# Turning the PSUM banks of a block's result, and converting weights in parts of 1024 columns: a state-space scan fused with two feed-forward layers

## The chip, the cores and the metric

The kernel runs on one core of one Trainium2 chip. The metric is the device time of one execution in microseconds (us). TensorE is called PE below, VectorE DVE, ScalarE ACT, GpSimd POOL, and SP is the engine that issues the DMAs.

## The reference, cut to what matters

```
# 1. scan over 4 sequences x 8 heads, 768 tokens each, in chunks of 32 tokens
L  = exp(cum_i - cum_j) * causal;  M = (C @ B.T) * L
y  = M @ x + (C @ state) * exp(cum)          # state is carried from chunk to chunk
# 2. two feed-forward layers on 3072 tokens x 256
h = x @ w_in;  g = maximum(0.01*h, h);  x   = g @ w_out       # 256 -> 2048 -> 256
h = x @ w_in2; g = maximum(h, 0);       out = (g * g) @ w_out2
```

The outputs are fp32. The eight-byte weights are handed over as they lie in memory and turned into fp32 pairs on the chip.

## The kernel before, in words

The 3072 tokens are cut into 12 **pieces** of 256. Each piece is scanned (`scan_piece`): DVE and ACT scale and decay the inputs, PE makes the small products S and Y, SP spreads four tiles into block-diagonal form by DMA (L321: `kbd`, `xbh`, `xbl`, `sbd`), and at the end ACT and DVE write the piece's result as a high and a low part, `yh` (L400) and `yl` (L401).

The two layers work on **blocks** (`Phase`) in the order of the table ORDER: six blocks of layer 1 with one piece each (256 columns), called blocks 0 to 5 here, then nine blocks with two pieces each (512 columns) of layers 2 and 1 by turns. A block has 16 slices of the 2048 hidden rows. For a one-piece block they go in 8 groups of two slices. A group is: `hmm`, 12 matmuls into a PSUM tile `hp` (L423 to L425, three buffers); `act`, which makes `gh` and its low part `gl` (L433, L434, L439); and `omm`, 12 matmuls into the block's result `o` (L451, L452, L456), two groups behind `hmm`. The result has two halves of 128 rows, d = 0 and 1. After a block of layer 1, `finish` copies each half to `yh` on ACT (L464) and subtracts for `yl` on DVE (L465). Until both are done, that half of `o` can't be written again.

Each product of fp32 values is three matmuls of high and low parts, so each weight matrix must be split once into a high and a low part. That is the **weight conversion**. A part of a matrix is loaded (L127, by SP), then goes through two ACT operations (L136, L139), two DVE operations (L147, L148), one ACT copy that makes the high part `wh` (L161) and one DVE subtraction that makes the low part `wl` (L162). In the code before, a part has 512 columns of eight-byte values (512 KB), the staging pool `wp` has 8 such buffers, and the steps `split_w`, `split_w1`, `split_w2` each run one part behind the other. Of the last matrix the low parts replace staging buffers (`w2o` tiles, from the same pool), and its last six parts have 256 columns and go through a single buffer called `all`, which the reductions over a sequence (L275, L277) use too.

Layer 1's weights (`1i` and `1o`) are converted on demand within block 0; from then on `w_step` is called `W_PACE` times a group. The order in which an engine's instructions stand is made by a scheduling layer out of the order of the calls and of the buffers that come free; each engine then runs its queue strictly in order. So an instruction that waits holds up all that stand behind it on its engine, on SP too.

Of the kernel before, what the change touches and what calls it, by code (L numbers as in the profile page):

```python
# [18 lines left out]
P = 128  # L19
BATCH, H, S, D, N = 4, 8, 768, 32, 16  # L20
T = 32
TP = 256
# [6 lines left out]
DM, FF = H * D, 2048  # L29
KI, KO = DM // P, FF // P  # L30
# [9 lines left out]

ENDS = [0, 12, 28, 44, 60, 76, 132, 156, 176, 216, 236, 280]
LAG = {1: 2, 2: 3}
W_AHEAD = 4
W_FROM, W_PACE = 16, 0.4


@with_exitstack
def ssd_moe_kernel(ctx: ExitStack, tc: tile.TileContext, in1, in2, w1i, w1o, w2i, w2o, out):
# [6 lines left out]
    nc = tc.nc  # L55

    cp = ctx.enter_context(tc.tile_pool(name="cp", bufs=1))
    sp = ctx.enter_context(tc.tile_pool(name="sp", bufs=1))
    sm = ctx.enter_context(tc.tile_pool(name="sm", bufs=2))
    wp = ctx.enter_context(tc.tile_pool(name="wp", bufs=8))  # L60
    yp = ctx.enter_context(tc.tile_pool(name="yp", bufs=2))
    ap_ = ctx.enter_context(tc.tile_pool(name="ap", bufs=2))
    ph = ctx.enter_context(tc.tile_pool(name="ph", bufs=3, space=bass.MemoryType.PSUM))
    po = ctx.enter_context(tc.tile_pool(name="po", bufs=1, space=bass.MemoryType.PSUM))
    pz = ctx.enter_context(tc.tile_pool(name="pz", bufs=1, space=bass.MemoryType.PSUM))


# [30 lines left out]
    w_last = {}  # L98
# [3 lines left out]

    def w_out(nm, m, c):
        if nm == "2o":
            t = w_last[m // 2]
            return t[:, 0, m % 2, c], t[:, 1, m % 2, c]
        return w_hi[nm][:, m, c], w_lo[nm][:, m, c]


    wq = [(nm, c, None) for c in range(8) for nm in ("1i", "1o")]  # L110
    wq += [("2i", c, None) for c in range(8)] + [("2o", c, None) for c in range(5)]
    wq += [("2o", c, j) for c in range(5, 8) for j in range(2)]
    w_loaded, w_half, w_full, w_done = [], [], [], set()

    def load_w():
        nm, c, j = wq.pop(0)
        if nm[1] == "i":
            sl = (slice(None), slice(None), slice(c * 256, c * 256 + 256))
        elif j is None:
            sl = (slice(None), slice(2 * c, 2 * c + 2), slice(None))  # L120
        else:
            sl = (slice(None), slice(2 * c + j, 2 * c + j + 1), slice(None))
        if j is None:
            st = wp.tile([P, 2, 256], I64, tag="w", name="wst")
        else:
            st = sp.tile([P, 1, 256], I64, tag="all", name="wst")
        nc.sync.dma_start(st, w_dram[nm][sl])  # L127
        w_loaded.append((nm, c, j, sl, st))

    def split_w():  # L130
        nm, c, j, sl, st = w_loaded.pop(0)
        v = st.bitcast(I32).rearrange("p k (f two) -> p k f two", two=2)
        w0, w1 = v[:, :, :, 0], v[:, :, :, 1]


        nc.scalar.activation(w1.bitcast(F32), w1.bitcast(F32), AF.Copy, scale=2.0**-112)  # L136


        nc.scalar.activation(  # L139
            w0, w0.bitcast(U32), AF.Copy, scale=2.0**-29 * (1 - 2.0**-14), bias=7.5 * 2.0**-14 - 0.5  # L140
        )
        w_half.append((nm, c, j, sl, w0, w1))

    def split_w1():

        nm, c, j, sl, w0, w1 = w_half.pop(0)
        nc.vector.scalar_tensor_tensor(w0, w1, 3, w0, ALU.logical_shift_left, ALU.bitwise_or)  # L147
        nc.vector.scalar_tensor_tensor(w0, w1, -(1 << 31), w0, ALU.bitwise_and, ALU.bitwise_or)  # L148
        w_full.append((nm, c, j, sl, w0.bitcast(F32)))

    def split_w2():

        nm, c, j, sl, w = w_full.pop(0)
        if nm == "2o":
            if c not in w_last:
                w_last[c] = wp.tile([P, 2, 2, 256], F32R, tag="w", name="w2o")
            k = slice(0, 2) if j is None else slice(j, j + 1)
            h, l = w_last[c][:, 0, k], w_last[c][:, 1, k]
        else:
            h, l = w_hi[nm][sl], w_lo[nm][sl]  # L160
        nc.scalar.activation(h, w, AF.Copy)  # L161
        nc.vector.tensor_tensor(l, w, h.bitcast(F32), ALU.subtract)  # L162
        if j != 0:
            w_done.add((nm, c))

    def w_step():
        if w_full:
            split_w2()
        if w_half:
            split_w1()  # L170
        if w_loaded:
            split_w()
        if wq:
            load_w()
# [8 lines left out]
    def load_piece(p):  # L183
        v = sp.tile([P, U * (N + T + D)], F32, tag="in1", name="in1")
        w = sp.tile([P, U * 2 * T], F32, tag="in2", name="in2")
        nc.sync.dma_start(v, in1[p])
        nc.sync.dma_start(w, in2[p])
        return part(v, N + T, D), part(v, 0, N), part(w, T, T), part(v, N, T), part(w, 0, T), part(w, 0, T + N)
# [215 lines left out]
    class Phase:  # L404
# [38 lines left out]
        def omm(self, ms):  # L443
            n = self.n
            if self.o is None:
                self.o = [po.tile([P, 512], F32, tag=f"o{d}", name=f"o{d}")[:, :n] for d in range(2)]
            gs = [self.g.pop(m) for m in ms]
            for m, (gh, gl) in zip(ms, gs):
                for d in range(2):
                    wh, wl = w_out(self.wo, m, slice(d * P, d * P + P))  # L450
                    nc.tensor.matmul(self.o[d], wl, gh, start=(m == 0), stop=False)  # L451
                    nc.tensor.matmul(self.o[d], wh, gh, start=False, stop=False)  # L452
            for m, (gh, gl) in zip(ms, gs):
                for d in range(2):
                    wh, _ = w_out(self.wo, m, slice(d * P, d * P + P))
                    nc.tensor.matmul(self.o[d], wh, gl, start=False, stop=(m == KO - 1))  # L456

        def finish(self):
            n = self.n
# [25 lines left out]
    loaded = {0: load_piece(0)}  # L485
    for _ in range(W_AHEAD):
        load_w()
# [32 lines left out]
    def second(lag):  # L520
        while len(pend) > lag:
            ph_, ms = pend.pop(0)
            ph_.omm(ms)
            if ms[-1] == KO - 1:
                ph_.finish()
# [3 lines left out]
    for layer, p0, n in ORDER:  # L529
        g, o = divmod(p0, 2)  # L530
        ph_ = Phase(layer, p0, n, *(t[:, o : o + n] for t in ys[g]))
        for m in range(0, KO, 2 // n):
            ms = list(range(m, m + 2 // n))
            while (ph_.wo, m // 2) not in w_done:
                w_step()
            ph_.hmm(ms)
            pos += 2
            ph_.act(ms)
            step_to(due(pos))
            pend.append((ph_, ms))  # L540
            second(LAG[n])
            if pos >= W_FROM:
                acc += W_PACE
            while acc >= 1:
                acc -= 1
                w_step()
# [52 lines left out]
```

## Time and profile before

| | |
|---|---|
| time, median of 3 runs (range) | 653.15 us (650.84 to 655.68) |
| profiled execution, its own time | 652.62 us |
| its span, first to last instruction | 650.8 us |
| PE busy | 595.4 us, 91% of the span, 4248 matmuls |
| DVE busy | 422.6 us, 65% |
| ACT busy | 358.9 us, 55% |
| HBM read and written | 36.83 MB and 3.15 MB |

How to read it: the shares are means over very different stretches. In the first 40 us the PE has little to do; from about 240 us on it is busy nearly without a break, while DVE and ACT have slack; between lies the stretch in which scans, weight conversion and the one-piece blocks share DVE and ACT. The times of single instructions and waits come from views of the same execution.

### The profile page before, as it was taken

What the parts mean: (1) busy time and instruction counts of PE and PEld (TensorE: products, weight loads), DVE (VectorE), ACT (ScalarE), POOL (GpSimd) and SP (SyncE); (2) the same over time, 40 slices, a digit from 0 to 9 for tenths busy, and PEclk for the clock granted to TensorE, in tenths of its full rate; (3) what the DMA queues carried; (4) which work ended last, traced back from release to release, by engine and by line L of the source; (5) the groups of instructions that cost most, each with busy time, mean ns of one, the idle gap of its engine ahead of it and who ended that gap; (6) DMA issues with size and microseconds to landing.
All of it is one profiled execution on the core that took longest, in us unless ns stands there. A gap on an engine that the chain in (4) does not pass through costs nothing.

```text
span 650.8 us, 10980 instructions
## 1 busy us (share of the span) xinstructions
PE 595.4 (91%) x4248; PEld 508.0 (78%) x4248; DVE 422.6 (65%) x735; ACT 358.9 (55%) x639; POOL 5.1 (1%) x14
## 2 busy tenths in 40 slices
PE   0276978899999999999999999999999999999997
PEld 0276868899999978888878888878888888788885
DVE  7998889899676587567673676652465322544553
ACT  5986867686555545555554455553444433544442
POOL 3000000000000000000000000000000000000000
PEclk9998879899999999999999999999999999999999
DMA  9647664633633423022332022030000000000000
GB/s 335 213 84 227 206 147 133 184 39 97 132 92 70 125 70 48 9 74 50 57 82 56 33 26 49 33 63 3 1 10 1 26 7 0 1 1 1 34 0 32
DMA packets 111251, 46.45 MB, mean 71 GB/s; under 512 B 94304, under 2 KB 100064, under 8 KB 111200
## 3 DMA queue, kind: packets, MB, share of 16 engines
q1 hardware_dynamic: 111200, 45.76, 27.6%
q8 instruction: 33, 0.54, 0.3%
q14 instruction: 18, 0.15, 0.1%
HBM read 36.83 MB, written 3.15 MB: 61 GB/s over the span
## 4 chain that ended last, share of the span: by engine, by line
PE 72%; DVE 14%; ACT 5%; DMA 5%; issue 3%; SPq 1%; DVEq 0%; ACTq 0%
PE o L451 12%; PE hp L423 12%; PE hp L424 11%; PE hp L425 11%; PE o L452 11%; PE o L456 11%; DMA wst<-w2o 2%; DVE gl L439 2%; DVE lt L199 1%; DMA all<-in 1%; DMA in<-in 1%; DVE wst L147 1%; DVE e L205 1%; DVE wst L148 1%; ACT gh L433 1%
## 5 line engine op out<-in xcount | busy, mean ns | idle before, releaser
L439 DVE TENSOR_TENSOR gl<-t,gh 128x512 fp32r<-128x512 f32 x192 | 132.3, 689 | 133.9 <-ACT t L434 80.5
L433 ACT ACTIVATE gh<-hp 128x512 fp32r<-128x512 f32 x96 | 57.2, 596 | 91.8 <-PE o L452 67.2
L423 PE MATMUL hp<-yl,wh1i 128*128 128x256 f32 (+1 forms) x288 | 95.9, 333 | 10.3 <-DVE yl L401 6.8
L438 ACT CAST gh<-t 128x512 fp32r<-128x512 f32 x96 | 59.6, 621 | 68.9 <-DVE t L437 53.8
L451 PE MATMUL o<-gh,wl1o 128*128 128x256 f32 (+1 forms) x288 | 90.1, 332 | 6.3 <-DVE yl L465 3.5
L437 DVE TENSOR_TENSOR t<-t 128x512 f32<-128x512 f32 x96 | 66.1, 689 | 45.5 <-ACT t L436 45.2
L425 PE MATMUL hp<-yh,wl1i 128*128 128x256 f32 (+1 forms) x288 | 94.3, 327 | 0.0
L424 PE MATMUL hp<-yh,wh1i 128*128 128x256 f32 (+1 forms) x288 | 94.1, 327 | 0.0
L436 ACT ACTIVATE t<-hp 128x512 f32<-128x512 f32 x96 | 57.4, 598 | 59.6 <-PE hp L425 57.3
L452 PE MATMUL o<-gh,wh1o 128*128 128x256 f32 (+1 forms) x288 | 88.8, 327 | 0.0
L451 PE MATMUL o<-gh,w2o 128*128 128x512 f32 x192 | 76.4, 398 | 1.3 <-DVE yl L465 1.3
L423 PE MATMUL hp<-yl,wh2i 128*128 128x512 f32 x192 | 76.2, 397 | 0.0
L425 PE MATMUL hp<-yh,wl2i 128*128 128x512 f32 x192 | 75.6, 394 | 0.0
L424 PE MATMUL hp<-yh,wh2i 128*128 128x512 f32 x192 | 75.5, 393 | 0.0
L452 PE MATMUL o<-gh,w2o 128*128 128x512 f32 x192 | 74.8, 389 | 0.0
L423 PEld LDWEIGHTS hp<-yl,wh1i 128*128 128x128 f32 x288 | 56.8, 197 | 15.7 <-DVE yl L401 7.0
L451 PEld LDWEIGHTS o<-gh,wl1o 128*128 128x128 f32 x288 | 56.0, 194 | 11.8 <-DVE yl L465 3.7
L456 PE MATMUL o<-gl,wh1o 128*128 128x256 f32 (+1 forms) x288 | 62.2, 323 | 0.5 <-DVE gl L439 0.5
L424 PEld LDWEIGHTS hp<-yh,wh1i 128*128 128x128 f32 x288 | 56.8, 197 | 4.4 <-issue 0.2
L456 PE MATMUL o<-gl,w2o 128*128 128x512 f32 x192 | 60.2, 393 | 0.0
L425 PEld LDWEIGHTS hp<-yh,wl1i 128*128 128x128 f32 x288 | 56.5, 196 | 4.4
L452 PEld LDWEIGHTS o<-gh,wh1o 128*128 128x128 f32 x288 | 56.0, 194 | 3.9
(124 smaller groups left out, 932.7 us busy)
## 6 DMA issues: line engine op xcount, KB each, us to landing
in<-in SPq DMA_DIRECT2D x12, 640.0 KB, 4.5
in<-in SPq DMA_DIRECT2D x12, 512.0 KB, 3.3
all<-in SPq DMA_DIRECT2D x15, 384.0 KB, 3.5
wst<-w1i SPq DMA_DIRECT2D x8, 512.0 KB, 6.7
wst<-w1o SPq DMA_DIRECT2D x8, 512.0 KB, 6.6
wst<-w2i SPq DMA_DIRECT2D x8, 512.0 KB, 4.7
out_t<-ob SPq DMA_DIRECT2D x12, 256.0 KB, 2.2
wst<-w2o SPq DMA_DIRECT2D x5, 512.0 KB, 5.1
```

The lines of the kernel that those rows point to most:

```text
L147: nc.vector.scalar_tensor_tensor(w0, w1, 3, w0, ALU.logical_shift_left, ALU.bitwise_or)
L423: nc.tensor.matmul(hp, wh, self.xl[:, :, k], start=(k == 0), stop=False)
L424: nc.tensor.matmul(hp, wh, self.xh[:, :, k], start=False, stop=False)
L425: nc.tensor.matmul(hp, wl, self.xh[:, :, k], start=False, stop=(k == KI - 1))
L433: nc.scalar.activation(gh, hp, AF.Lrelu)
L436: nc.scalar.activation(t, hp, AF.Relu)
L437: nc.vector.tensor_tensor(t, t, t, ALU.mult)
L438: nc.scalar.copy(gh, t)
L439: nc.vector.tensor_tensor(gl, t, gh.bitcast(F32), ALU.subtract)
L451: nc.tensor.matmul(self.o[d], wl, gh, start=(m == 0), stop=False)
L452: nc.tensor.matmul(self.o[d], wh, gh, start=False, stop=False)
L456: nc.tensor.matmul(self.o[d], wh, gl, start=False, stop=(m == KO - 1))
```

## The change

Four things are changed together.

1. A one-piece block's result no longer takes a 256-column half of each of two PSUM banks, but both halves of one bank. The pool `po` has one tag with two buffers, so blocks take the banks in turn. Only the first matmul into the bank has the start flag. A two-piece block still takes both banks, one for each half of the rows.
2. A weight part has 1024 columns (1 MB) instead of 512, but for the first four (columns 0 to 511 of `1i` and of `1o`), which keep 512, and for the last eight, which have 256. That makes 24 parts in place of 35. The pool `wp` has 4 buffers of double size, of which each of the first four parts fills half of one.
3. `split_w` and `split_w1` are one step, so the conversion has two steps a part.
4. Two parts are loaded ahead instead of four, and a `w_step` is called 0.3 times a group instead of 0.4.

```diff
-W_AHEAD = 4
-W_FROM, W_PACE = 16, 0.4
+W_AHEAD = 2
+W_FROM, W_PACE = 16, 0.3
...
-    wp = ctx.enter_context(tc.tile_pool(name="wp", bufs=8))
+    wp = ctx.enter_context(tc.tile_pool(name="wp", bufs=4))
...
-    po = ctx.enter_context(tc.tile_pool(name="po", bufs=1, space=bass.MemoryType.PSUM))
+    po = ctx.enter_context(tc.tile_pool(name="po", bufs=2, space=bass.MemoryType.PSUM))
...
-    wq = [(nm, c, None) for c in range(8) for nm in ("1i", "1o")]
-    wq += [("2i", c, None) for c in range(8)] + [("2o", c, None) for c in range(5)]
-    wq += [("2o", c, j) for c in range(5, 8) for j in range(2)]
-    w_loaded, w_half, w_full, w_done = [], [], [], set()
+    wq = [(nm, c, n) for c, n in ((0, 2), (2, 2), (4, 4), (8, 4), (12, 4)) for nm in ("1i", "1o")]
+    wq += [("2i", c, 4) for c in range(0, KO, 4)] + [("2o", 0, 4), ("2o", 4, 4)]
+    wq += [("2o", c, 1) for c in range(8, KO)]
+    w_loaded, w_half, w_done = [], [], set()
...
+        pool, tag, size = (sp, "all", 256) if n == 1 else (wp, "w", 1024)
+        st = pool.tile([P, size], I64, tag=tag, name="wst")[:, : 256 * n]
...
-        w_half.append((nm, c, j, sl, w0, w1))
-    def split_w1():
-        nm, c, j, sl, w0, w1 = w_half.pop(0)
         nc.vector.scalar_tensor_tensor(w0, w1, 3, w0, ALU.logical_shift_left, ALU.bitwise_or)
         nc.vector.scalar_tensor_tensor(w0, w1, -(1 << 31), w0, ALU.bitwise_and, ALU.bitwise_or)
-        w_full.append((nm, c, j, sl, w0.bitcast(F32)))
+        w_half.append((nm, c, n, sl, w0.bitcast(F32)))
...
     def w_step():
-        if w_full:
-            split_w2()
         if w_half:
-            split_w1()
+            split_w2()
...
-                self.o = [po.tile([P, 512], F32, tag=f"o{d}", name=f"o{d}")[:, :n] for d in range(2)]
+                o = [po.tile([P, 512], F32, tag="o", name="o") for _ in range(self.n // TP)]
+                self.o = [o[0][:, d * n : d * n + n] for d in range(2)] if n == TP else o
...
-                    nc.tensor.matmul(self.o[d], wl, gh, start=(m == 0), stop=False)
-                    nc.tensor.matmul(self.o[d], wh, gh, start=False, stop=False)
+                    f = m == 0 and (d == 0 or n > TP)
+                    nc.tensor.matmul(self.o[d], wl, gh, start=f, stop=False, skip_group_check=True)
+                    nc.tensor.matmul(self.o[d], wh, gh, start=False, stop=False, skip_group_check=True)
...
-            while (ph_.wo, m // 2) not in w_done:
+            while (ph_.wo, ms[-1]) not in w_done:
                 w_step()
```

The change moves instructions on every engine. In the rows below a line number of the changed kernel is 8 lower than before in the scan and 4 lower from `omm` on, so L351 of before is L343 now, L401 is L393, L465 is L461.

**PE, where block 0 ends and block 1 begins.** `hp` is the hidden tile, `o0`, `o1` (before) and `o_1096` (now) block 1's result, `kbd` and `S` belong to the scan of piece 2. Before:

```order
L424 MATMUL hp_1310<-yh_337,wh1i_110 128x256
L425 MATMUL hp_1310<-yh_337,wl1i_111 128x256
L451 MATMUL o0_1161<-gh_987,wl1o_113 128x256
L452 MATMUL o0_1161<-gh_987,wh1o_112 128x256
L351 LDWEIGHTS kbd_95
L351 MATMUL S_1050<-ch_950,kbd_95 128x32
```

Now:

```order
L416 MATMUL hp_1056<-yh_333,wh1i_110 128x256
L417 MATMUL hp_1056<-yh_333,wl1i_111 128x256
L447 MATMUL o_1096<-gh_930,wl1o_113 128x256
L448 MATMUL o_1096<-gh_930,wh1o_112 128x256
L447 MATMUL o_1096<-gh_930,wl1o_113 128x256
L448 MATMUL o_1096<-gh_930,wh1o_112 128x256
```

Before, block 1's result is begun after the hidden tiles of its first six groups, with the scan's S right behind. Now it is begun after three groups' hidden tiles, and results and hidden tiles alternate from there on.

**ACT, in the scan of piece 0, ahead of the first block.** `d1s` and `shl` carry the piece's states, `wst` are staging buffers of weight parts; `wst_395` is the part of `1o` for slices 4 to 7. Before:

```order
L136 ACTIVATE wst_365<-wst_365 128x512
L380 ACTIVATE d1s_233<-Y_240,kk_158 128x32x8
L161 ACTIVATE wh1o_112<-wst_126 128x512
L139 ACTIVATE wst_365<-wst_365 128x512
L385 CAST shl_296<-stt_290 128x16x16
```

Now:

```order
L136 ACTIVATE wst_357<-wst_357 128x1024
L139 ACTIVATE wst_357<-wst_357 128x1024
L372 ACTIVATE d1s_229<-Y_236,kk_154 128x32x8
L136 ACTIVATE wst_395<-wst_395 128x1024
L377 CAST shl_292<-stt_286 128x16x16
```

The first operation on `wst_395` now stands between `d1s` and `shl`, so `shl` waits for the landing of that part.

**DVE, the last rows ahead of `yl` of piece 2**, with which block 2 begins. Before:

```order
L147 SCALAR_TENSOR_TENSOR wst_893<-wst_893 128x512
L353 TENSOR_TENSOR e1_1454<-in1_1246,e1_1454 128x512
L344 SCALAR_TENSOR_TENSOR xl_1488<-in1_1246,sc_1149,xh_1451 128x512
L148 SCALAR_TENSOR_TENSOR wst_893<-wst_893 128x512
L215 MEMSET d1s_1576 128x32
L465 TENSOR_TENSOR yl_338<-o0_1161,yh_337 128x256
L334 SCALAR_TENSOR_TENSOR kmx_1444<-in2_1247,sc_1149,him_1396 128x512
L401 SCALAR_TENSOR_TENSOR yl_1362<-Y_1194,fac_945,yh_1361 128x512
```

Now:

```order
L345 TENSOR_TENSOR e1_1388<-in1_1188,e1_1388 128x512
L461 TENSOR_TENSOR yl_334<-o_1096,yh_333 128x256
L142 SCALAR_TENSOR_TENSOR wst_1115<-wst_1115 128x1024
L336 SCALAR_TENSOR_TENSOR xl_1422<-in1_1188,sc_1084,xh_1385 128x512
L143 SCALAR_TENSOR_TENSOR wst_1115<-wst_1115 128x1024
L326 SCALAR_TENSOR_TENSOR kmx_1378<-in2_1189,sc_1084,him_1338 128x512
L393 SCALAR_TENSOR_TENSOR yl_1296<-Y_1136,fac_888,yh_1295 128x512
```

Two conversions stand among these rows in both programs, of 512 columns before and of 1024 now; the second half of block 1's finish (L461) has moved ahead of `yl`.

## Rows read from the trace of the kernel before

**Rows 1.** The page, part 1: busy us, share of the span, instructions.
```profile
PE 595.4 (91%) x4248; PEld 508.0 (78%) x4248; DVE 422.6 (65%) x735; ACT 358.9 (55%) x639; POOL 5.1 (1%) x14
```

**Rows 2.** Stretches, us: busy PE, PEld, DVE, ACT, POOL; clock, DMA share, GB/s.
```profile
37.40:116.10 78.70, 64.01 (x616) 60.02 (x616) 71.48 (x140) 57.76 (x107) 0.00 (x0) 0.89 0.61 162
116.10:232.80 116.70, 111.15 (x1165) 107.74 (x1165) 92.66 (x167) 72.68 (x141) 0.00 (x0) 0.98 0.44 106
232.80:650.80 418.00, 413.69 (x2348) 335.11 (x2348) 225.53 (x346) 199.41 (x344) 0.00 (x0) 1.00 0.13 29
112.90:119.80 6.90, 3.67 (x17) 3.67 (x18) 6.31 (x13) 3.38 (x7) 0.00 (x0) 0.51 0.37 38
```

**Rows 3.** Waits of PE, 40 to 240 us: us in total, times, longest.
```profile
PE o L451 <- DVE yl L465: 4.8, 2, 3.5
PE hp L423 <- DVE yl L401: 4.0, 1, 4.0
...
PE o L451 <- DVE wl1o L162: 2.6, 2, 2.3
```

**Rows 4.** Timeline of PE: start us, us, instruction, idle before it.
```profile
37.37 0.58 PE L423 MATMUL hp<-yl,wh1i 128*128 128x256 f32 x1 [2.78 <-DVE yl L401]
...
90.10 0.58 PE L451 MATMUL o<-gh,wl1o 128*128 128x256 f32 x1 [3.54 <-DVE yl L465]
...
116.14 0.58 PE L423 MATMUL hp<-yl,wh1i 128*128 128x256 f32 x1 [4.02 <-DVE yl L401]
...
232.79 0.50 PE L451 MATMUL o<-gh,w2o 128*128 128x512 f32 x1 [1.25 <-DVE yl L465]
```

**Rows 5.** Busy time as in rows 2, `yl` of piece 0 to `yl` of piece 2.
```profile
36.57:115.33 78.76, 64.04 (x616) 60.05 (x616) 71.54 (x142) 57.94 (x108) 0.00 (x0) 0.90 0.62 163
```

**Rows 6.** Groups by line and shape, DVE, 37.4 to 115.2 us: count, busy us, mean ns.
```profile
L148 DVE SCALAR_TENSOR_TENSOR wst<-wst 128x512 int32<-128x512 int32 x16 | 10.5, 684 | 0.0
L147 DVE SCALAR_TENSOR_TENSOR wst<-wst 128x512 int32<-128x512 int32 x15 | 9.8, 681 | 0.0
...
L162 DVE TENSOR_TENSOR wl1o<-wst,wh1o 128x512 fp32r<-128x512 f32 x6 | 4.1, 690 | 2.7 <-ACT wh1o L161 2.6
```

**Rows 7.** Timeline of DVE: start us, us, instruction.
```profile
47.40 1.29 DVE L147 SCALAR_TENSOR_TENSOR wst<-wst 128x512 int32<-128x512 int32 x2
48.60 0.69 DVE L148 SCALAR_TENSOR_TENSOR wst<-wst 128x512 int32<-128x512 int32 x1
...
114.36 0.39 DVE L465 TENSOR_TENSOR yl<-o,yh 128x256 fp32r<-128x256 f32 x1
...
115.33 0.75 DVE L401 SCALAR_TENSOR_TENSOR yl<-Y,fac,yh 128x512 fp32r<-128x512 f32 x1
```

**Rows 8.** Groups by line and shape, the whole span, conversion at two sizes.
```profile
L136 ACT ACTIVATE wst<-wst 128x512 f32<-128x512 f32 x29 | 19.5, 674 | 1.7 <-DMA wst<-w1i 1.6
...
L136 ACT ACTIVATE wst<-wst 128x256 f32<-128x256 f32 x6 | 2.6, 442 | 5.6 <-DMA wst<-w2o 5.6
...
L148 DVE SCALAR_TENSOR_TENSOR wst<-wst 128x256 int32<-128x256 int32 x6 | 2.5, 424 | 0.1
```

**Rows 9.** Waits of DVE, 36.6 to 115.3 us: us in total, times, longest.
```profile
DVE wl1o L162 <- ACT wh1o L161: 2.6, 3, 1.5
DVE m L293 <- PE S L290: 2.0, 1, 2.0
```

**Rows 10.** Timeline of ACT in the scan of piece 0.
```profile
29.33 0.66 ACT L385 CAST shl<-stt 128x256 f16<-128x256 f32 x1 [0.80 <-DVE stt L223]
```

**Rows 11.** Timeline of SP's queue: a load of `1o`.
```profile
20.83 0.33 SPq L127 DMA_DIRECT2D wst<-w1o  x1
```

**Rows 12.** The page, part 6: DMA issues, KB each, median us to landing.
```profile
in<-in SPq DMA_DIRECT2D x12, 640.0 KB, 4.5
...
wst<-w1o SPq DMA_DIRECT2D x8, 512.0 KB, 6.6
wst<-w2i SPq DMA_DIRECT2D x8, 512.0 KB, 4.7
```

More of the change, by code (lines that the diff above doesn't have):

```diff
@@ L104, in w_out @@
         if nm == "2o":
-            t = w_last[m // 2]
-            return t[:, 0, m % 2, c], t[:, 1, m % 2, c]
+            t = w_last[m // 4]
+            return t[:, 0, m % 4, c], t[:, 1, m % 4, c]
         return w_hi[nm][:, m, c], w_lo[nm][:, m, c]
-    wq = [(nm, c, None) for c in range(8) for nm in ("1i", "1o")]
-    wq += [("2i", c, None) for c in range(8)] + [("2o", c, None) for c in range(5)]
-    wq += [("2o", c, j) for c in range(5, 8) for j in range(2)]
-    w_loaded, w_half, w_full, w_done = [], [], [], set()
+    wq = [(nm, c, n) for c, n in ((0, 2), (2, 2), (4, 4), (8, 4), (12, 4)) for nm in ("1i", "1o")]
+    wq += [("2i", c, 4) for c in range(0, KO, 4)] + [("2o", 0, 4), ("2o", 4, 4)]
+    wq += [("2o", c, 1) for c in range(8, KO)]
+    w_loaded, w_half, w_done = [], [], set()
     def load_w():
-        nm, c, j = wq.pop(0)
+        nm, c, n = wq.pop(0)
+        pool, tag, size = (sp, "all", 256) if n == 1 else (wp, "w", 1024)
+        st = pool.tile([P, size], I64, tag=tag, name="wst")[:, : 256 * n]
         if nm[1] == "i":
-            sl = (slice(None), slice(None), slice(c * 256, c * 256 + 256))
-        elif j is None:
-            sl = (slice(None), slice(2 * c, 2 * c + 2), slice(None))
-        else:
[L122 to L126, printed above, removed]
+            st = st.rearrange("p (k f) -> p k f", k=KI)
+            sl = (slice(None), slice(None), slice(c * P, (c + n) * P))
+        else:
+            st = st.rearrange("p (k f) -> p k f", f=DM)
+            sl = (slice(None), slice(c, c + n), slice(None))
         nc.sync.dma_start(st, w_dram[nm][sl])
-        w_loaded.append((nm, c, j, sl, st))
+        w_loaded.append((nm, c, n, sl, st))
     def split_w():
-        nm, c, j, sl, st = w_loaded.pop(0)
+        nm, c, n, sl, st = w_loaded.pop(0)
         v = st.bitcast(I32).rearrange("p k (f two) -> p k f two", two=2)
@@ L141, in split_w @@
         )
-        w_half.append((nm, c, j, sl, w0, w1))
-    def split_w1():
-        nm, c, j, sl, w0, w1 = w_half.pop(0)
         nc.vector.scalar_tensor_tensor(w0, w1, 3, w0, ALU.logical_shift_left, ALU.bitwise_or)
         nc.vector.scalar_tensor_tensor(w0, w1, -(1 << 31), w0, ALU.bitwise_and, ALU.bitwise_or)
-        w_full.append((nm, c, j, sl, w0.bitcast(F32)))
+        w_half.append((nm, c, n, sl, w0.bitcast(F32)))
     def split_w2():
-        nm, c, j, sl, w = w_full.pop(0)
+        nm, c, n, sl, w = w_half.pop(0)
         if nm == "2o":
[L155 to L158, printed above, removed]
+            g, o = divmod(c, 4)
+            if g not in w_last:
+                w_last[g] = wp.tile([P, 2, 4, DM], F32R, tag="w", name="w2o")
+            h, l = w_last[g][:, 0, o : o + n], w_last[g][:, 1, o : o + n]
         else:
@@ L162, in split_w2 @@
         nc.vector.tensor_tensor(l, w, h.bitcast(F32), ALU.subtract)
-        if j != 0:
-            w_done.add((nm, c))
+        w_done.update((nm, m) for m in range(c, c + n))
     def w_step():
-        if w_full:
+        if w_half:
             split_w2()
-        if w_half:
-            split_w1()
         if w_loaded:
@@ L455, in omm @@
                     wh, _ = w_out(self.wo, m, slice(d * P, d * P + P))
-                    nc.tensor.matmul(self.o[d], wh, gl, start=False, stop=(m == KO - 1))
+                    nc.tensor.matmul(self.o[d], wh, gl, start=False, stop=(m == KO - 1), skip_group_check=True)
         def finish(self):
```

## The prediction

> **What bounds the kernel now.** I read the busy times first, then stretches, then the PE's waits, then the queue of the engine that ends them. PE is busy 595.4 us of 650.8 [rows 1]. From 232.8 us to the end it is busy 413.69 of 418.00 at a granted clock of 1.00, and the last 4 us are the final copy and store [rows 2]; nothing in the change touches that stretch. From 116.1 to 232.8 us it is busy 111.15 of 116.70. So only two places can give much: the time before the first block, and the stretch from 37.4 to 116.1 us, blocks 0 and 1, where PE is busy 64.01 of 78.70 us and the clock is 0.89.
>
> In that stretch DVE is busy 71.48 of 78.70, so PE is not its bound. The PE's waits say the same: the largest end with DVE's `yl`, 4.0 us on the scan's (L401) and 4.8 us on the finish's (L465), and 2.6 us with DVE's `wl1o` [rows 3]. Single rows place them: at 90.10 us PE has stood 3.54 us for block 0's finish, at 116.14 it has stood 4.02 us for piece 2's `yl`, at 232.79 it has stood 1.25 us for block 5's finish [rows 4]. By 116.14 PE has run out of everything: blocks 0 and 1 are complete, and block 2 needs piece 2. **So the wait that ends last is `yl` of piece 2**, an instruction in DVE's queue, and what PE gains earlier it loses there. The change is worth what it does to the time of that instruction, plus what it does after it.
>
> **Part 1, the banks in turn.** The 3.54 us at 90.10 go: block 1 no longer needs block 0's bank. What is late next is piece 2's `yl`, so by itself this buys nothing, except through DVE: one idle wait of DVE, 2.0 us for `m` from PE's S (L290) [rows 9], came about because that S stood in PE's queue behind block 1's `omm`, which stood still. I count these 2.0 us as gained. The order of PE supports it: `omm` of block 1 now follows its third group.
>
> A wait is added: both halves lie in one bank now, and the order shows the second ACT copy (L464 for d = 1) waiting for the first DVE subtraction, which it didn't. Behind it on ACT stand the next group's `gh` and `t`. It happens six times, a copy and a subtraction late at most, and up to block 4 PE has another bank to go on with: zero, with at most 0.8 us on the other side. Block 5 is followed by a two-piece block, which takes both banks, one of them block 5's; its 1.25 us [rows 4] may go or double, and I leave them.
>
> **Part 2, larger parts, on DVE.** Between `yl` of piece 0 and `yl` of piece 2 lie 78.76 us, of which DVE is busy 71.54 and idle 7.2 [rows 5]. Conversion takes 15 + 16 + 15 instructions of 512 columns there (of the last 15, 6 stand in the row of `wl1o` and 9 in two like it) [rows 6]. Back to back they begin 0.60 us apart (47.40, 48.60 after two [rows 7]), so 46 x 0.60 = 27.6 us. In the order of the changed kernel 8 + 9 + 9 = 26 of 1024 columns stand there: because a part comes whole, and because the parts run further ahead, more of the conversion falls before piece 2. A larger one is priced from two sizes: 424 ns at 256 columns [rows 8] and 684 at 512 [rows 6], 260 for 256 more, so 684 + 520 = 1204 ns, and 1.12 us from one to the next by the same overlap of 0.08. 26 x 1.12 = 29.1, which is **1.5 us more**. Between these two points the changed order also has one scan instruction of 512 columns (`cl`) that stood before, 0.67 us by the row of L401 less the overlap, one more half of a finish, 0.31 us (both [rows 7]), and five of one or three columns, 0.5 us together as an estimate from the shortest half above. **Sum: 3.0 us more for DVE.**
>
> Against it stands the idle time. The 2.0 us of part 1 go. The 2.6 us in which DVE waited for ACT's `wh1o` [rows 9] should go too, since ACT has less to do: at 674 and 442 ns for 512 and 256 columns [rows 8] one of 1024 takes 1138, 210 less than two, and each subtraction now has a longer one of another part ahead of it to hide the copy. That is -4.6, with 2.6 us of idle time kept. Bounds: none of the 7.2 goes (+3.0 net), or all (-4.2 net).
>
> **Part 3, the first block's start.** Before, `shl` runs on ACT at 29.33 [rows 10] and block 0 begins at 37.37 [rows 4]. Now the first operation on `wst_395`, 1.14 us, stands ahead of `shl`. Its load goes into the buffer of another part of `1o` and can be issued when that part's `wl` is done, at the place where SP issued its next `1o` load before, 20.83 [rows 11]. It holds `shl` up once it lands after 29.33 - 1.14 = 28.2, that is once it takes over 7.4 us. Loads of 512 KB took 4.7 and 6.6 us, one of 640 KB 4.5 [rows 12]. So 1 MB takes from 4.7 (no slower than half of it) to 13.2 (two of the slow ones in a row), which costs 0 to 5.8 us. I take 8.0, between the slow 6.6 and twice 4.7: **0.6 us**. The Trainium skill (DMA: Bandwidth & Descriptors, Bandwidth) gives 6.15 us for one load of 1 MB from HBM. By that the part would land at 27.0, this term would be 0 and the sum 0.6 lower. Its fit in the section on a DMA's anatomy, 2.0 us plus the bytes at 436 GB/s, makes 3.2 us of 512 KB; the trace has 4.7 and 6.6, so I don't use it.
>
> The rest of the DVE's queue ahead of the first `yl` changes by less than 0.3 us: three more conversions of 512 columns, 1.6 net after merging, come in; one `wl` (0.60), `cl` (0.67) and five short ones go out.
>
> **Part 4, afterwards.** From 116.1 to 232.8 DVE is busy 92.66 of 116.70 and PE idle 5.55 [rows 2]. The last eight parts cost three more short instructions each way and the earlier ones less: zero, bounded by those 5.55 us below and by 1 us above. Fewer steps called (0.3 a group) do no harm: twelve steps bring 12 parts until the first two-piece block, which covers all of `2i` and most of `2o`.
>
> **Sum:** +3.0 - 4.6 + 0.6 = -1.0 us on the profiled execution's 652.62 (a span of 650.8 and 1.8 around it): **651.6 us**. That execution lies 0.5 below the median of the three runs, 653.15, well within their 650.84 to 655.68. About 1% (6.5 us) is what I take as distinguishable from no change.
>
> **Rivals.**
>
> *DVE's queue closes up.* All 7.2 us of idle time go, so -4.2; block 2 begins without PE standing still long before it, so the low clock behind that wait (0.51 from 112.9 to 119.8 [rows 2]; 3.67 us of PE's work at half speed) gives 1.8 back; the 1.25 us at 232.79 go, and half of the other 4.3 us of PE's idle time after 116.1. -9.4 in all: 643.2. For it: one cause, PE standing before L465, is removed, and idle time on DVE comes from PE. Against: PE has slack all through this stretch, so DVE's queue alone must shorten.
>
> *ACT stands before loads of 1 MB* (slower). The place is `shl`; it decides from a landing time over 7.4 us. At 9.4 to 13.2 us it costs 2.0 to 5.8, in the middle 3.9 on block 0's start. The later parts of `1o` then land late as well and the 2.6 us on `wh1o` stay: 3.0 - 2.0 + 3.9 = +4.9, so 657.5. For it: 512 KB took 6.6 us here. Against: fewer loads share the engines at the start.
>
> *The banks only move the wait.* PE waits at 116 in place of 90 and the conversions come out even: 652.6.
>
> *The clock.* In blocks 0 and 1 the granted clock is 0.89, and it is 0.51, the lower of its two levels (1.2 GHz) nearly throughout, in the 6.9 us around PE's wait of 4.02 us [rows 2, 4]. If at each of the five borders between one-piece blocks PE waited briefly so that the clock fell in the same way, each would cost the 1.8 us worked out above, 9 in all: 660.6. The Trainium skill (TensorE: Matmul & The Clock Gate, A second HAM failure mode) tells of a kernel whose cycling through PSUM banks made short PE gaps between groups and the clock swing. The trace here speaks against it: the hidden tiles turn through three banks from 232.8 us on and the clock stays at 1.00 [rows 2].
>
> **Chances.** Forecast 0.45, the queue closes up 0.20, ACT before loads 0.20, the wait only moves 0.11, the clock 0.04. Faster by over 1% (below 646.6) is most of the second and a tail of the first: 0.19. Slower by over 1% (above 659.7) is the clock and the upper third of the third: 0.13. The rest, 0.68, is within 1%. The range reaches down to 644, which cuts off the lower half of the fast rival, and up to 659, which cuts off the clock and the latest landings. The forecast alone, by its bounds of -4.2 and +3.0 and runs 1.5 us apart either way, would be 647 to 657.
>
> **What would show it.** Right: no wait of PE for L465 near 90 us, one for L401 near 115; conversions of 1024 columns near 1.2 us on DVE and 1.14 on ACT; DVE idle about 2.6 us between the two `yl`; `shl` within a microsecond of 29.3. Wrong: ACT idle before L136 with a DMA as its releaser, or block 0 beginning after 39 us (the load's rival); block 2 beginning before 112 us (the queue closing up); low clock at block borders behind 120 us.

## The result, and the profile after

| | before | after |
|---|---|---|
| time, median (range), runs | 652.25 us (650.84 to 655.68), 4 | 660.34 us (659.10 to 660.74), 4 |
| profiled execution, its span | 652.62, 650.8 us | 660.56, 658.8 us |

The ratio is 1.0113 [1.0069, 1.0157]; run again later it was 1.0117 [1.0091, 1.0143]. The change makes the kernel 1.1% slower, 7.4 us by this ratio; the forecast was 651.6 in a range of 644 to 659, no change. Two executions, one of e10 (3256 us) and one of e13 (754.5 us), took far longer than all others of their kernels and are left out of the ratios.

The page of the changed kernel, part 1, answers to [rows 1]: PE has about as much to do as before.

```profile
PE 597.3 (91%) x4248; PEld 510.4 (77%) x4248; DVE 421.9 (64%) x702; ACT 356.4 (54%) x606; POOL 5.1 (1%) x14
```

Stretches of it, with the columns of [rows 2]: blocks 0 and 1; block 2 to the wait at 241.48; the rest; `yl` of piece 0 to `yl` of piece 2, as [rows 5]; and two stretches of low clock.

```profile
37.40:117.95 80.55, 63.13 (x616) 59.64 (x617) 74.72 (x129) 61.06 (x89) 0.00 (x0) 0.89 0.63 173
117.95:241.48 123.53, 114.89 (x1168) 111.25 (x1169) 90.70 (x157) 69.36 (x135) 0.00 (x0) 0.95 0.41 94
241.48:658.80 417.32, 412.72 (x2344) 334.37 (x2344) 223.70 (x343) 199.20 (x344) 0.00 (x0) 1.00 0.13 28
36.62:117.06 80.44, 63.13 (x616) 59.61 (x616) 74.61 (x129) 60.95 (x90) 0.00 (x0) 0.90 0.62 173
110.40:124.10 13.70, 7.16 (x61) 7.12 (x62) 11.90 (x16) 7.35 (x14) 0.00 (x0) 0.50 0.49 76
192.30:199.20 6.90, 4.69 (x19) 4.02 (x20) 2.97 (x11) 0.97 (x2) 0.00 (x0) 0.51 0.37 73
```

The last stretch is as long as before (418.00), the first 1.85 us longer (78.70), the middle one 6.8 longer (116.70). So in these two executions most of the loss lies behind block 2's start, where the forecast had put zero. PE's larger waits in the execution after the change:

```profile
112.53 0.18 PE L388 MATMUL Y<-qh,sbd 128*128 128x32 f16 x1 [4.10 <-DMA sbd<-t]
...
117.95 0.55 PE L415 MATMUL hp<-yl,wh1i 128*128 128x256 f32 x1 [4.41 <-DVE yl L393]
...
194.51 0.38 PE L282 MATMUL S<-ident,mx 128*3 128x128 f32 x1 [4.52 <-DVE mx L269]
...
241.48 0.47 PE L447 MATMUL o<-gh,w2o 128*128 128x512 f32 x1 [1.77 <-DVE yl L461]
```

The wait at 90.10 of [rows 4] is gone, and block 2 starts 1.81 us later (117.95 for 116.14). Block 5's border (241.48) has 1.77 us in place of 1.25. New is 194.51: the S of sequence 2's reduction (L282), which finds the scales of pieces 6 to 8. Before, the same matmul (L290) waited 0.72 us:

```profile
198.23 0.27 PE L290 MATMUL S<-ident,mx 128*3 128x128 f32 x1 [0.72 <-DVE mx L277]
```

Its operand did not come later than before: the reduction that it waits for began at 197.22 us before and at 193.50 after, so it came 3.7 us earlier. PE came to it earlier still. In PE's order it stands behind 935 block matmuls (`hmm` and `omm`) before and behind 867 after, 68 fewer, and PE stands until the reduction arrives. The reduction in its turn waited for a load:

```profile
193.50 0.95 DVE L269 TENSOR_REDUCE mx<-all 128x1 f32<-128x768 f32 x1 [1.51 <-DMA all<-in]
```

SP issued that load at 189.84, as the reduction ahead of it (188.89 to 189.82) had freed the one buffer `all`. So the wait before S has two sides, PE's early arrival and this chain of load and reduction through one buffer. Only the first was varied below; a second buffer for `all` was not tried.

From these rows the two profiled executions differ by: block 2's start, 1.8; the low clock behind it, to 124.1 against 119.8 before, at half speed (124.1 - 117.95) / 2 - (119.8 - 116.14) / 2 = 1.2; the wait for S, 4.52 - 0.72 = 3.8; the low clock behind S, 4.69 / 2 = 2.3; together 9.1, of which PE's other waits from block 2's start to 241 us give 0.7 back. The spans differ by 8.0; about half a microsecond stays unexplained.

### The profile page after: what moved, and what is told of

Same layout as the page of the kernel before. It is cut to its first block, busy times and chain, and to the rows that moved or that the text cites. A ratio compares the mean times of both kernels' runs of the same rounds, so it can differ in the third digit from the quotient of the medians.

```text
span 658.8 us, 10902 instructions
## 1 busy us (share of the span) xinstructions
PE 597.3 (91%) x4248; PEld 510.4 (77%) x4248; DVE 421.9 (64%) x702; ACT 356.4 (54%) x606; POOL 5.1 (1%) x14
## 4 chain that ended last, share of the span: by engine, by line
PE 72%; DVE 11%; DMA 7%; ACT 4%; issue 3%; SPq 2%; DVEq 0%; ACTq 0%
PE hp L415 12%; PE hp L417 12%; PE hp L416 12%; PE o L447 12%; PE o L452 11%; PE o L448 11%; DMA all<-in 2%; DMA in<-in 2%; SPq L313 2%; DVE gl L431 1%; DMA wst<-w1o 1%; DMA wst<-w2o 1%; DVE lt L191 1%; DVE e L197 1%; ACT t L426 1%
## 5 line engine op out<-in xcount | busy, mean ns | idle before, releaser
L416 PE MATMUL hp<-yh,wh1i 128*128 128x256 f32 (+1 forms) x288 | 95.6, 332 | 0.0
```

Of the source, the lines that this page charges most:

```text
L416: nc.tensor.matmul(hp, wh, self.xh[:, :, k], start=False, stop=False)
```

## Experiments

Ratios are to the kernel before, run on the same chip in turns with each kernel (its median there was 652.6 to 653.4). The runs are from three chips; differences between kernels below are differences of these ratios. Each run's kernel has line numbers of its own. The theories: A, PE stands before S of sequence 2 and the clock is low behind it; B, turning the banks costs by itself; C, whatever wait is removed, the next late thing takes its place; D, DVE's longer queue ahead of piece 2's `yl` delays block 2. "Place of S" is the number of block matmuls ahead of S of sequence 2 in PE's order.

| run | part size | banks | place of S | time, us | ratio [95%] |
|---|---|---|---|---|---|
| e1 | 512 | in turn | 918 | 652.88 | 0.9999 [0.9979, 1.0020] |
| e2 | 1024 | as before | 862 | 658.35 | 1.0100 [1.0084, 1.0117] |
| e3 | 1024 | in turn | 804, constant | 657.14 | 1.0065 [1.0044, 1.0085] |
| e4 | 512 | as before | 804, constant | 655.06 | 1.0037 [1.0025, 1.0049] |
| e5 | 1024 | in turn | 948 | 654.42 | 1.0038 [1.0011, 1.0065] |
| e7 | 512 | in turn | 948 | 649.47 | 0.9941 [0.9915, 0.9967] |
| e9 | 512, merged steps | in turn | 948 | 650.89 | 0.9979 [0.9957, 1.0001] |
| e10 | 512 | as before | 948 | 650.25 | 0.9958 [0.9939, 0.9977] |
| e13 | 1024, last two matrices 512 | in turn | 948 | 653.04 | 1.0004 [0.9980, 1.0027] |
| e14 | 512, last two matrices 1024 | in turn | 948 | 663.88 | 1.0182 [1.0155, 1.0210] |
| e15 | 512, merged steps | in turn | 886 | 654.49 | 1.0032 [1.0009, 1.0054] |
| e16 | the changed kernel | | 867 | 659.52 | 1.0117 [1.0091, 1.0143] |

### One part of the change alone (e1, e2)

e1 is the kernel before with the banks' lines of the diff alone; e2 is the changed kernel with them undone:

```diff
-    po = ctx.enter_context(tc.tile_pool(name="po", bufs=2, space=bass.MemoryType.PSUM))
+    po = ctx.enter_context(tc.tile_pool(name="po", bufs=1, space=bass.MemoryType.PSUM))
...
-                self.o = [o[0][:, d * n : d * n + n] for d in range(2)] if n == TP else o
+                self.o = [po.tile([P, 512], F32, tag=f"o{d}", name=f"o{d}")[:, :n] for d in range(2)]
```

> The kernel before with the banks in turn alone; parts of 512 columns, pace and steps as before. Theory A (the lost time is PE standing in its queue before the reduction matmul S of sequence 2, which the change put 68 matmuls of the blocks earlier, 867 ahead of it instead of 935, and the low clock behind that wait): here 918 stand ahead of S, so the wait there grows from 0.7 us to 2 to 3 and no low clock need follow; block 2 begins 1 to 2 us earlier than 116.1; time 651 to 654. Theory B (turning the banks itself costs, by making the copies of a block's end serial on ACT and DVE and by letting PE run dry before block 2): most of the 8 us is here, 657 to 660.

> The changed kernel with the result in two banks without turns, as before; parts of 1024 columns, pace and steps as changed. Theory A: 862 matmuls of the blocks stand ahead of S of sequence 2, so PE stands there 4 us or more and the low clock follows; DVE carries 3 us more before block 2 and still waits for block 0's finish, so block 2 begins at 117 to 119; time 659 to 662. Theory B: close to the kernel before, 652 to 655.

The banks alone change nothing, the parts alone bring 1.0% of the 1.1%. Rows of PE in e1's profiled execution:

```profile
114.83 0.58 PE L423 MATMUL hp<-yl,wh1i 128*128 128x256 f32 x1 [4.90 <-DVE yl L401]
...
196.93 0.27 PE L290 MATMUL S<-ident,mx 128*3 128x128 f32 x1 [2.24 <-DVE mx L277]
```

Block 2 starts 1.3 us earlier than before, then S, moved up by 17 matmuls, is waited for 2.24 us in place of 0.72, and the clock is low from 198.7 to 202.1. That the banks won the 1.3 us is not shown: block 2's start differs by more between executions with the same order (116.14 before and 112.50 in e10, below).

### S without its wait (e3, e4)

```diff
+        if s == 2:
+            mx = sm.tile([P, 5], F32, tag="mc", name="mc", bufs=1)
+            nc.gpsimd.memset(mx, 0.5)
```

ahead of `powers` in `sequence_scales`, in the changed kernel (e3) and in the one before (e4).

> The changed kernel, in which the reduction matmul of sequence 2 reads a constant 0.5 in place of the maxima (loads and reductions are still made, their result is left unused). So PE can't stand before S for the last reduction. Theory A: the 4.5 us wait near 190 us and the low clock from 192 to 199 go, 4.5 + 2.3 = 6.8 less than the changed kernel: about 653.5. Theory C (PE is simply early there, and the next thing late, the scan of piece 5 or 6, takes the wait over): 659 to 660.

> The kernel before with the same constant for sequence 2, as a control. Theory A: the wait there was 0.7 us and the clock stayed high, so 651 to 652. If the constant helps in another way (DVE's order, S earlier), it would show here as more than 2 us.

The wait for S goes, 3 us come back, about half of what theory A said. The constant is no clean tool: it lets S rise to 804 and costs the kernel before 2.4 us, where 651 to 652 was expected. And in e3 PE stands next for the scan's own product:

```profile
195.20 0.18 PE L391 MATMUL Y<-qh,sbd 128*128 128x32 f16 x1 [2.09 <-DMA sbd<-t]
```

### S moved later (e5, e7, e10, e15, e16)

The reduction's data comes as early as ever; only its S and what follows are called within piece 6's scan:

```diff
+QN[6] += 6
...
+        for _ in range(10 if s == 2 else 0):
+            yield
         sc, isc, sbp = yield from powers(mx)
...
-            for _ in bd:
+            for _ in bd if p != 5 else ():
                 pass
             yield p
+            for _ in range(6 if p == 5 else 0):
+                next(bd, None)
+                yield p
```

e5 is the changed kernel with it, e7 the banks alone, e10 the kernel before. e15 and e16, without it, stand here as their counterparts.

> The changed kernel, with the S matmul of sequence 2's reduction moved later on PE, behind 948 block matmuls instead of 867 (the same work; piece 6's scan starts a few steps later). Theory A (the wait of PE before S, 4.5 us, and the low clock behind it, 192 to 199 us, are what the larger parts cost after block 2's start): both go, and the time is 653 to 655. Theory D (DVE's 3.0 us more before piece 2 is the other half: block 2 starts 1.8 us later and has 3.1 us less at full clock): the S wait goes, block 2 still starts near 118, and the time is 656 to 658. Theory C (the next late thing takes the wait): another wait of over 2 us between 185 and 215 and 659 to 661.

> Banks in turn alone (parts of 512 as before), with S of sequence 2 behind 948 block matmuls instead of 918. If the bank turn's gain was given back to the S wait (2.24 us) and the low clock behind it (198.7 to 202.1, 1.7 us), the time falls from 652.9 to 649 to 650 and is 2 to 4 us below the kernel before. If the gain never was there, 652 to 653.

> The kernel before with S of sequence 2 behind 948 block matmuls instead of 935, where PE waited 0.72 us: 652 to 653. With the banks in turn and the same S the time was 649.5; if that gain is the banks', this one stands 3 us above it and has the wait of 3.5 us near 89 for the old half of the result. If the later S alone gave it, it is 649 to 650.

> The changed kernel with parts of 512 (8 buffers, 4 ahead, 0.4 steps a group), S where the order puts it, behind 886 block matmuls. If the place of S costs by itself, PE stands for 3 to 4 us before S, the clock is low behind it, and the time is 655 to 657, 5 above the same kernel with S behind 948 (650.9). If S costs only together with the large parts, it is 651 to 652.

> The changed kernel itself, on the chip of the three others: 659 to 661. Against it and the kernel before, each theory's share can be taken from one chip.

Later S makes every kernel faster: e16 to e5 by 0.79% (5.2 us), e15 to e9 by 0.53% (3.5), e1 to e7 by 0.58% (3.8), before to e10 by 0.42% (2.7). In e5 S starts without waiting, and a shorter wait for `sbd` (L391) is left:

```profile
117.14 0.55 PE L418 MATMUL hp<-yl,wh1i 128*128 128x256 f32 x1 [4.41 <-DVE yl L396]
...
192.68 0.18 PE L391 MATMUL Y<-qh,sbd 128*128 128x32 f16 x1 [2.75 <-DMA sbd<-t]
...
202.32 0.38 PE L285 MATMUL S<-ident,mx 128*3 128x128 f32 x2
```

against e16, the changed kernel again:

```profile
192.17 0.37 PE L282 MATMUL S<-ident,mx 128*3 128x128 f32 x1 [4.98 <-DVE mx L269]
```

So moving S is shown to pay, in its size theory A (653 to 655). But the move does more than take S's wait away. PE's wait at block 5's border (1.25 us before, 1.77 and 1.44 in the two executions of the changed kernel, 1.28 in e15) is gone with S late in e5, e9 and e10, and 0.60 in e7. In the executions shown this accounts for what the kernel before gains behind block 2's start: from there to the end it takes 534.66 us (650.8 - 116.14) and e10 532.70 (645.2 - 112.50), 1.96 less, and the two waits that are gone, 0.72 and 1.25, make 1.97. Nor was e15 what was expected, 3 to 4 us before S and 655 to 657: PE stood there 3.23 us for `sbd` and then only 0.38 for S. Only the difference of the moves, 5.2 - 2.7 = 2.5 us, is the change's. e10 also takes the banks' gain away: with S late they are worth 0.17%, 1.1 us, inside the intervals (my expectation of 652 to 653 for e10 fell). e7 is the fastest kernel here, 0.6% faster than before.

### PE kept busy before block 2 (e6, e8)

```diff
+    def warm(p, w, v, n):
+        if p == 2:
+            hp = ph.tile([P, 512], F32, tag="h", name="warm")
+            for _ in range(n):
+                nc.tensor.matmul(hp[:, 0:TP], w, v[:, 0:NC], start=True, stop=True)
...
+        warm(p, t16[:, 0:4], qh, 30)
         for u in range(U):
...
+        warm(p, sbd[:, 0], qh, 30)
```

in e5 (e6), and with 16 and 34 in e7 (e8).

> The kernel of the run before (S behind 948), with 60 idle matmuls of 128x256 (fp16, into a hidden tile that the block overwrites) on PE, 30 ahead of the scan products with sbd of piece 2 and 30 behind them, where PE stood for 4.1 and 4.4 us ahead of block 2. They wait for nothing later than the work around them and should be done before the data comes. If the low clock from 110 to 124 us follows from PE's standing there, block 2 runs at full clock from its start near 118, and the time is 2.5 to 3 us below the run before. If the clock falls all the same, the times of the two are equal within 1 us; if the idle matmuls hold the path up, it is slower by up to 3 us.

> The run before (banks in turn alone, S behind 948), with 16 idle matmuls ahead of and 34 behind piece 2's products with sbd, where PE stood for 2.5 and 4.9 us. Block 2's start at 114.8 then meets full clock instead of a low one up to 120.2 (2.7 us): 646 to 648, the fastest so far. If standing PE is not what lowers the clock there: as the run before, 649 to 650.

Both are slower by over 5 us than e5 and e7, where 2.5 to 3 us less was expected: 659.63 (1.0093 [1.0060, 1.0126]) and 658.17 (1.0069 [1.0043, 1.0095]). In e6:

```profile
108.92 0.39 PE L310 MATMUL warm<-qh,t 128*128 128x256 f16 x1 [4.81 <-DVE t L390]
...
117.71 0.37 PE L426 MATMUL hp<-yl,wh1i 128*128 128x256 f32 x1
```

```profile
118.00:140.00 22.00, 21.30 (x236) 20.55 (x234) 20.79 (x35) 15.96 (x31) 0.00 (x0) 1.00 0.38 84
```

With PE busy ahead of it, block 2 runs at a clock of 1.00 from its start, where e5 has 0.50 to 121.3. The price can't be read from it: the scheduling layer moved the end of block 1 behind block 2's start (block 1's last finish begins at 130.4 us instead of 112.3), and the wait of 4.8 us stayed, ahead of the idle matmuls. These took 8.4 us of PE, and the end of block 1 was still to do behind them: from block 2's start to the end e6 takes 539.6 us and e5 534.8.

### Part size (e9, e13, e14)

e9 is e5 with parts of 512 (the steps stay merged); e9 also has 8 buffers of half the size, 4 loads ahead and 0.4 steps a group. e14 has the first line of this diff alone (4 loads ahead), e13 the second alone (0.4 steps a group).

```diff
-    wq = [(nm, c, n) for c, n in ((0, 2), (2, 2), (4, 4), (8, 4), (12, 4)) for nm in ("1i", "1o")]
-    wq += [("2i", c, 4) for c in range(0, KO, 4)] + [("2o", 0, 4), ("2o", 4, 4)]
+    wq = [(nm, c, n) for c, n in ((c, 2) for c in range(0, KO, 2)) for nm in ("1i", "1o")]
+    wq += [("2i", c, 2) for c in range(0, KO, 2)] + [("2o", c, 2) for c in range(0, 8, 2)]
```

> The changed kernel with parts of 512 columns again (8 buffers, 4 ahead, 0.4 steps a group; the last eight parts of 256 stay), but the two merged conversion steps, the banks in turn, and S of sequence 2 behind 948 block matmuls. If the size of the parts is what costs 5 us against the banks alone with the same S (654.4 against 649.5), the time is 649 to 650 and block 2 starts near 114. If it is the merged steps, it is 653 to 655 and block 2 starts near 117.

> The changed kernel with S behind 948 (654.4 before), and parts of 512 for the last two matrices alone; w1i and w1o keep 1024. If wide operations in front of piece 2's yl are what costs, the time falls to 651 and the stretch from the yl of piece 1 to that of piece 2 shortens. If it is the wide operations of w1i and w1o in block 0, the yl of piece 1 stays near 76 (39 us behind that of piece 0), block 2 starts near 117, and the time stays 654 to 655.

> The reverse: parts of 512 for w1i and w1o (4 loads ahead, in the 4 large buffers), 1024 for the last two matrices, S behind 948. If block 0's wide operations cost the 4 us, the yl of piece 1 comes near 71, block 2 starts near 113 to 114, and the time is 650 to 651. If those of w2i do, it is 654 to 655. Both could share it: then both kernels stand near 652.5.

Rows as in [rows 5], `yl` of piece 0 to `yl` of piece 2, of e5, e9, e13 and e14:

```profile
36.75:116.25 79.50, 61.89 (x616) 58.23 (x616) 74.41 (x130) 61.25 (x90) 0.00 (x0) 0.92 0.63 175
```

```profile
36.39:112.37 75.98, 61.89 (x616) 58.04 (x616) 71.81 (x143) 58.55 (x107) 0.00 (x0) 0.92 0.66 172
```

```profile
36.65:114.26 77.61, 65.02 (x616) 61.90 (x616) 71.15 (x134) 54.97 (x91) 0.00 (x0) 0.89 0.57 147
```

```profile
37.12:121.69 84.57, 65.83 (x616) 61.71 (x616) 77.81 (x141) 63.70 (x103) 0.00 (x0) 0.86 0.65 189
```

The fourth number is DVE's busy time. Small parts, with their buffers, loads ahead and pace, take 2.6 us off DVE there (74.41 to 71.81) and 3.5 off the stretch, and the time falls by 0.59%, 3.9 us. The split by matrix has no clean answer: e13 gets back 2.2 us, no more than its interval. e14, expected at 650 to 651, is the slowest of all: with four loads ahead, conversions of 1024 columns of `2i` move in front of piece 2's `yl`, DVE has 6 us more than in e9, and PE stands 6.24 and 4.35 us ahead of block 2, at 122.49. It was not the test that I meant, but its extra DVE time comes back in the stretch and more (8.6 us).

### Less work for DVE (e11, e12)

e5 and e7 with most of `w2i`'s conversion on DVE left out; a sixteenth of each part is kept in e11 and an eighth in e12 (the expectation gives these fractions too high):

```diff
+        q = slice(0, 32 if nm == "2i" else None)
-        nc.vector.tensor_tensor(l, w, h.bitcast(F32), ALU.subtract)
+        nc.vector.tensor_tensor(l[..., q], w[..., q], h.bitcast(F32)[..., q], ALU.subtract)
```

and the same `q` on the two operations of `split_w`; `wl2i` is filled with zeros on POOL at the start.

> The changed kernel with S behind 948, of which DVE converts only an eighth or a quarter of each part of w2i (the rest is left out, so its time is a lower bound). Between the yl of pieces 0 and 2 DVE has some 7 us less. Theory D (DVE's queue ahead of piece 2's yl sets block 2's start): block 2 starts at 110 to 112 instead of 117.1, and the time is 646 to 649 against 654.4. If the scan's own chain or PE sets it, block 2 starts after 115 and the time is above 652.

> The same w2i work left out with the banks alone and parts of 512 (S behind 948): block 2 starts near 110 instead of 114.0, and the time is 645 to 647 against 649.5. Theory D: the parts' 5.0 us between the two kernels shrink to 2 or less once DVE is light; otherwise the difference stays 4 to 5.

655.96 (1.0050 [1.0026, 1.0075]) and 655.12 (1.0032 [1.0012, 1.0052]): both expectations of time failed. Block 0 begins some 3 us later (at 40.43 and 40.19; 37.54 in e5). The fill is POOL's last instruction, so nothing on POOL waits behind it. But while it runs, DVE's scaling of piece 0's inputs takes 3.24 us in e11 and ends as the fill does; in e5, without the fill, it took 0.41 (why is not shown):

```profile
5.83 3.51 POOL L98 MEMSET wl2i<- 128x4096 f32 x1
6.39 3.24 DVE L192 TENSOR_SCALAR in<-in 128x496 f32<-128x496 f32 x1
```

```profile
6.51 0.41 DVE L189 TENSOR_SCALAR in<-in 128x496 f32<-128x496 f32 x1
```

e11's stretch from `yl` to `yl`:

```profile
39.66:116.17 76.51, 62.35 (x616) 59.27 (x616) 65.69 (x130) 58.55 (x86) 0.00 (x0) 0.92 0.60 165
```

DVE is busy 8.7 us less than in e5, but the stretch is only 3.0 shorter and DVE idle 10.8 us: in this execution something else sets its length, and block 2 does not start at 110 to 112. In e12 the scheduling layer put other conversions in the freed place, of `w2o` among them (62 conversion instructions stand there, 47 in e7), DVE is busy 70.43 us, only 1.4 less than in e7, and nothing is gained. The two kernels are 0.18% apart, 1.2 us, where e5 and e7 are 0.97%; but both got slower, e12 by far more, and DVE is not light in e12, so this says nothing for theory D.

## Why the prediction was wrong, step by step

**Two steps failed: part 4, "afterwards: zero", bounded by 1 us of loss, and the -4.6 us of idle time in part 2.**

**Part 4** weighed how much DVE and PE have to do behind 116 us and did not follow PE's order there. In it S of sequence 2 stands 68 matmuls further up. PE stood 4.5 and 5.0 us before it in the two profiled executions, and the clock was low for 6.9 and 6.8 us, from within the wait to behind it. Moving S later gives back 5.2 us of the changed kernel and 2.7 of the one before: the term is 2.5 us net (the intervals make it uncertain by about 2.7, so it is not clear of zero, and the move takes the wait at block 5's border with it).

With S late in both kernels the changed one is still 0.80% slower, 5.2 us (e5 against e10, uncertain by 2.2). So by these medians the place of S is the smaller share; the larger belongs to the parts and their steps, which part 2 priced at 3.0 us and then set 4.6 us of idle time against.

**In part 2 the busy term was right, the idle term wrong.** Forecast were +3.0 us of DVE; 74.61 - 71.54 is 3.07. The rows of the larger conversions came out as worked out:

```profile
L143 DVE SCALAR_TENSOR_TENSOR wst<-wst 128x1024 int32<-128x1024 int32 x9 | 10.9, 1216 | 0.0
...
L157 DVE TENSOR_TENSOR wl1o<-wst,wh1o 128x1024 fp32r<-128x1024 f32 x3 | 3.7, 1225 | 1.7 <-ACT wh1o L156 1.7
```

But of the -4.6 for idle time little came. The waits for `wh1o` stayed (1.7 us for 2.6), and new ones appeared, the longest for `t` on ACT:

```profile
DVE wl1o L157 <- ACT wh1o L156: 1.7, 3, 1.1
DVE gl L431 <- ACT t L426: 1.5, 2, 1.3
```

Worse, the 7.2 us that I meant to shrink were no property of the kernel. PE, DVE, ACT and SP have the same order in e10 as before up to block 2, and its execution shows

```profile
36.52:111.69 75.17, 61.36 (x616) 57.31 (x616) 71.25 (x141) 58.35 (x108) 0.00 (x0) 0.94 0.63 171
```

that is the same busy time and 3.9 us idle. The changed kernel has 5.8 us in one execution and 3.6 (77.98 - 74.35) in the other. Idle time varies by 2 to 3 us from execution to execution; the busy time varies by 0.3. The forecast should have taken +3.0 without the gain against it. With the 2.5 us of S that makes 5.5 of the 7.6 us. With larger parts DVE's queue is longer where block 2 waits for its end; the last rows ahead of piece 2's `yl` show two conversions of 1.2 us in the place of two of 0.7:

```profile
113.47 1.21 DVE L142 SCALAR_TENSOR_TENSOR wst<-wst 128x1024 int32<-128x1024 int32 x1
114.60 0.74 DVE L336 SCALAR_TENSOR_TENSOR xl<-in,sc,xh 128x512 f16<-128x512 f32 x1
115.27 1.22 DVE L143 SCALAR_TENSOR_TENSOR wst<-wst 128x1024 int32<-128x1024 int32 x1
116.40 0.74 DVE L326 SCALAR_TENSOR_TENSOR kmx<-in,sc,him 128x512 f16<-128x512 f32 x1
117.06 0.74 DVE L393 SCALAR_TENSOR_TENSOR yl<-Y,fac,yh 128x512 fp32r<-128x512 f32 x1
```

At one place of S part size, with its buffers, loads ahead and pace, costs 3.9 us (e5 to e9, uncertain by 2.3). What the two steps of the conversion cost besides (merged steps, with eight last parts instead of six) is e9 to e7, 2.5 us, uncertain by 2.2 and not looked into. The forecast had no term for it.

**Part 1 was right in its mechanism**: the wait at 90 us goes, the next late thing is piece 2's `yl`, and the banks by themselves buy nothing (e1: 0.9999; with S late -1.1 us). Its 2.0 us of DVE are not seen in the time. In e1, too, PE stands for that `yl`, so the wait has only moved. The serial reads of the two halves cost little.

So the loss splits into S 2.5, part size 3.9, merged steps 2.5 and banks -1.1, each uncertain by 2 to 3 us. That they add up to the measured 7.6, but for rounding, is no check: they are differences along one chain of runs (e16, e5, e9, e7, e10, before), and such a chain always adds up.

**Part 3's mechanism was right, and its price was hidden.** ACT did wait for the 1 MB load, as the forecast said, and `shl` began where it did before ([rows 10], 29.33). That was luck: DVE's `stt`, for which `shl` waited before, was done at 28.45, 0.8 us earlier than before, and `shl` stood behind L136 until 29.32. So the load cost some 0.9 us, which the earlier `stt` paid for, and the forecast had no term for that.

```profile
28.29 1.16 ACT L136 ACTIVATE wst<-wst 128x1024 f32<-128x1024 f32 x1 [0.82 <-DMA wst<-w1o]
29.32 0.66 ACT L377 CAST shl<-stt 128x256 f16<-128x256 f32 x1
```

```profile
27.72 0.73 DVE L215 TENSOR_TENSOR_SCAN stt<-dec,d1s 128x288 f32<-128x288 f32 x1
```

Issued at 20.89, the part had landed by 28.29, 7.4 us, at the threshold that the forecast named. That is more than the 6.15 us of the Trainium skill (DMA: Bandwidth & Descriptors, Bandwidth), which the medians over all such loads bracket. The two are not quite the same thing: its figure is the time that the transfer kept the DMA busy, and the times here run from issue to landing:

```profile
wst<-w2i SPq DMA_DIRECT2D x4, 1024.0 KB, 5.5
wst<-w1i SPq DMA_DIRECT2D x3, 1024.0 KB, 5.8
wst<-w1o SPq DMA_DIRECT2D x3, 1024.0 KB, 5.0
...
wst<-w2o SPq DMA_DIRECT2D x2, 1024.0 KB, 6.8
```

**The rivals.** "The clock" gave 660.6, near the result by coincidence: there was no price at five borders between blocks, but more low clock behind block 2's wait (1.2 us) and the 2.3 behind S. Turning through the banks, which its sentence from the Trainium skill (TensorE: Matmul & The Clock Gate, A second HAM failure mode) is about, did not bring it: e1 turns them and is no slower. DVE's queue did not close up, and ACT did not hold up block 0. "The banks only move the wait" was right about the wait (117.95 in place of 90.10) and wrong about the conversions, which did not come out even.

## What to carry to other kernels

Before a term "afterwards: nothing" is written, look up in the new order where the one-off instructions stand on the engine that sets the end (a reduction's matmul, a scale, a transpose): an in-order queue that reaches one of them 68 matmuls earlier stands for it, even when its data come sooner. Ask, too, what that instruction's data wait for; here it was a load through a single buffer. Take an instruction's duration from one execution, but not the idle time between instructions: look at a second execution before planning to win it back. And a knob of the scheduling layer (part size, loads ahead, filler, work left out) moves other work too, so an experiment shows what it was meant to show only if the order beside it stays as it was.

## What the runs showed of the hardware

Around waits of PE, and on behind them while PE worked, the granted clock was at the lower of its two levels (0.50, which is 1.2 of 2.4 GHz), and how long did not follow from the length of the wait alone. In the changed kernel it was low from 110.4 to 124.1 us, around two waits of 4.10 and 4.41 us, and from 192.3 to 199.2, around one of 4.52. But with a wait of 4.10 us in e2 it was low for 3.4 us (193.3 to 196.7), and with one of 4.81 us in e6, where idle matmuls followed, for 3.5 us (108.6 to 112.1). With single waits of 2.75 us in e5 and of 1.70 us in e12 it was low for 3.4 us (193.0 to 196.4, 194.4 to 197.8), with one of 1.87 us in e7 not at all. So the wait of 4.5 us before S cost another 2.3 us behind its end.

In e11 and e12 two short DVE instructions ran at the same time as a fill on POOL (5.83 to 9.34 us in e11). They took 3.07 and 3.24 us in e11, where e5, without the fill, has 0.17 and 0.41.
